# Decode step of two attention-and-MLP layers: extra matmuls over a resident weight at the end of each layer, and one key load cut in two

## The chip, the cores and the metric

The kernel runs on one core of a Trainium2 chip. The metric is device time in microseconds (us) of one execution. TensorE (PE) multiplies, VectorE (DVE) and ScalarE (ACT) work on vectors, GpSimd (POOL) does one small power, SyncE (SP) and ScalarE also issue DMAs. PSUM is the memory that matmuls write; everything else on the core lies in SBUF.

## The reference

One token of width 640 passes twice through the same two blocks, with the same weights and the same cache:

```python
x = x + A_ref(layernorm(x))     # 32 heads of 128 over 8192 cached keys and values, then wo
x = x + B_ref(layernorm(x))     # relu(x @ w1) @ w2, width 1728
x = x + A_ref(layernorm(x))
x = x + B_ref(layernorm(x))
```

`A_ref` is `q = x @ wq` (640 by 4096), scores `q . k * 128**-0.5`, a softmax over the 8192 keys of each head, the weighted sum of the values, and the product with `wo` (4096 by 640). All is float32. The cache is 32 heads x 8192 x 128 x 4 bytes, twice (keys and values): 268 MB. It doesn't fit in SBUF, so it is read from HBM in both layers.

## The kernel before

**Layers and heads.** `attention_and_mlp(L, xr, s)` runs twice. Layer 0 takes the heads from 0 to 31, layer 1 from 31 to 0, so that the last heads of layer 0 are the first of layer 1. What heads 30 and 31 left in SBUF (all of head 31, most of head 30) is used again without a load.

**Ring.** Keys and values go through one SBUF tile, `ring`. `UNITS` says in which units a head is loaded: most heads as one unit of keys and one of values (4 MB each), heads 1 and 29 in halves (2 MB), head 31 in halves of keys and smaller pieces of values. A unit of keys holds runs `(r, 0, 512)` of `K_ALL`, four of them per head. `pump` (L126) issues loads on SP's queue strictly in the order of `todo`, each as soon as `place` finds room for it; `release` frees the room of a piece when its matmuls have been issued, and the load's issue then waits on SP until these matmuls are done. When layer 0 ends, the ring is full of kept pieces and nothing can be loaded until layer 1 has used the first of them. The head that layer 1 loads first is head 29, then head 28. The rest of head 30's keys goes into two weight tiles that are free by then (`load_beside`, L140).

**One head.** `scores` (L336) multiplies four column strips of the array at once: 16 matmuls of 512 columns for a head. Then come the softmax on DVE and ACT, `turn` (L357, transposes by matmul), `rows_weighed` (L370, L377), `values` (L391, again 16 matmuls) and `output` (L415). A float32 matmul shows in the trace as two records.

**End of a layer.** After the last head's `output`, one chain runs that nothing overlaps: the last column times the hidden-layer weights and `wo` (L477, L304), copies to SBUF, turning rows into columns with small matmuls (L643, L656, L664), `deviations` (L261) for the second layer norm, 40 matmuls over `w2` (L304), of which DVE does the first block itself (L651, L684), `spread_of_rows` (L274, then L217 and the power on POOL), and the new `x` (L700). In layer 0 the next layer's `centred` (L232 to L246), `spread_of_columns` (L256), `queries` (L284 to L299) and the first scores follow. In layer 1 the output is stored (L709).

**Order.** The order of instructions on each engine is that of the code. Each engine takes its instructions in turn, and semaphores hold an instruction until its operands are ready. Side jobs (queries of the next group, `wo` of the last, products of `w1` with the last head's rows of `wo`, L464) are generators that are advanced between pieces. `ps_m` gives one PSUM buffer for each name (`pm`, `pt`, `px`, `acc`).

Of the kernel before, what the change touches and what calls it, by code (L numbers as in the profile page):

```python
# [10 lines left out]
F32 = mybir.dt.float32  # L11
# [4 lines left out]
P = 128  # L16
# [19 lines left out]
K_ALL = [(r, 0, RUN) for r in range(4)]  # L36
V_ALL = [(b, 0, 4) for b in range(NBL)]
WHOLE = [("k", K_ALL), ("v", V_ALL)]
HALVES = [("k", K_ALL[:2]), ("k", K_ALL[2:]), ("v", V_ALL[:2]), ("v", V_ALL[2:])]
LAST = [("v", V_ALL[:2]), ("v", V_ALL[2:3]), ("v", [(3, 0, 3)]), ("v", [(3, 3, 1)])]  # L40
UNITS = {h: WHOLE for h in range(H)}
UNITS[0] = HALVES[:2] + LAST
UNITS[1] = HALVES
UNITS[29] = HALVES
UNITS[30] = [
    ("k", [(0, 432, 80), (1, 0, 80)]),
    ("k", [(0, 0, 432)]),
# [25 lines left out]
def decode_kernel(ctx: ExitStack, tc: tile.TileContext, x, kv, wq, wo, w1, w2, out):  # L73
    nc = tc.nc
# [3 lines left out]
    ps_m = ctx.enter_context(tc.tile_pool(name="ps_m", bufs=1, space=bass.MemoryType.PSUM))  # L78
# [88 lines left out]
    def load_wq(g, queue):  # L167
        wq_t[g] = wts.tile([P, NB, HG * DH], F32, name="wq_t")
        queue.dma_start(wq_t[g], wq[g])
# [5 lines left out]
    xr = work.tile([P, DR], F32, name="xr", bufs=2)  # L175
# [14 lines left out]
    ident = consts.tile([P, P], F32, name="ident")  # L190
# [11 lines left out]
    w1_t = consts.tile([P, NB, DFF], F32, name="w1_t")  # L202
# [12 lines left out]
    def inv_std(ss):  # L215
        v = work.tile([P, 1], F32, name="ln_v")
        nc.vector.tensor_scalar(v, ss, 1.0 / D, EPS, op0=ALU.mult, op1=ALU.add)  # L217
        r = work.tile([P, 1], F32, name="ln_r", bufs=2)
        nc.gpsimd.tensor_tensor(r, v, mhalf, op=ALU.pow)
        return r  # L220

    def at_once(steps):
        while True:
            try:
                next(steps)
            except StopIteration as e:
                return e.value

    def centred(xt, s):

        pt = ps_m.tile([P, 512], F32, name="pm")
        nc.tensor.matmul(pt[:, :4], xt[:, :P], sel[:, :4], start=True, stop=True)  # L232
        for g in range(4):
            nc.tensor.matmul(
                pt[32 * g : 32 * g + 32, 4:5],
                xt[:, P:],
                sel[:, g : g + 1],
                start=True,
                stop=True,
            )  # L240
        nc.tensor.matmul(pt[:, 5:6], all_rows, s, start=True, stop=True)
        yield "dve"
        m = work.tile([P, 1], F32, name="ln_m")
        nc.vector.tensor_scalar(m, pt[:, 5:6], 1.0 / D, 0.0, op0=ALU.mult, op1=ALU.add)
        xc = work.tile([P, NB], F32, name="ln_xc", bufs=2)
        nc.vector.tensor_scalar(xc, pt[:, :NB], m, 0.0, op0=ALU.subtract, op1=ALU.add)  # L246
        return xc

    def spread_of_columns(xc):
        sq = work.tile([P, NB], F32, name="ln_sq")  # L250
        ss = work.tile([P, 1], F32, name="ln_ss")
        nc.vector.scalar_tensor_tensor(
            sq, xc, 1.0, xc, op0=ALU.mult, op1=ALU.mult, accum_out=ss
        )
        pv = bank_tile()[:, :1]
        nc.tensor.matmul(pv, ss.to_broadcast([P, P]), ones, start=True, stop=True)  # L256
        return inv_std(pv)
# [14 lines left out]
    def spread_of_rows(ss):  # L272
        pv = ps_m.tile([P, 512], F32, name="pm")
        nc.tensor.matmul(pv[:, :1], all_rows, ss, start=True, stop=True)  # L274
        return inv_std(pv[:, :1])

    qT = {}

    def queries(g, xc, r):

        pq = ps_m.tile([P, 512], F32, name="px")
        for c in range(NB):
            for j in range(HG):
                nc.tensor.matmul(  # L284
                    pq[32 * j : 32 * j + 32, :DH],
                    xc[:, c : c + 1].to_broadcast([P, 32]),
                    wq_t[g][:, c, j * DH : (j + 1) * DH],
                    start=(c == 0),
                    stop=(c == NB - 1),
                )  # L290
        yield "dve"
        row = work.tile([P, DR], F32, name="q_row")[:, :DH]
        nc.vector.tensor_scalar(row, pq[:, :DH], r[0], SCALE, op0=ALU.mult, op1=ALU.mult)
        yield "pe"
        pt = ps_m.tile([P, 512], F32, name="px")
        nc.tensor.matmul(pt[:, :HG], row, sel[:, :HG], start=True, stop=True)  # L296
        yield "dve"
        qT[g] = work.tile([P, HG], F32, name="qT", bufs=2)
        nc.vector.tensor_copy(qT[g], pt[:, :HG])  # L299

    def times_rows(acc, wt, col, first, last):

        for g in range(4):
            nc.tensor.matmul(  # L304
                acc[32 * g : 32 * g + 32, :DR],
                col.to_broadcast([col.shape[0], 32]),
                wt[:, g * DR : (g + 1) * DR],
                start=first,
                stop=last,
                skip_group_check=True,  # L310
            )
# [91 lines left out]
    def output(hd, col):  # L403

        oc = work.tile([P, 5, DH], F32, name="p")
        pt = ps_m.tile([P, 512], F32, name="pm")
        if hd.out is hd.out_3:
            nc.vector.tensor_copy(oc[:, :2], hd.out[:, :2])  # L408
            nc.scalar.copy(oc[:, 2:4], hd.out[:, 2:])  # L409
        else:  # L410
            nc.vector.tensor_copy(oc[:, :3], hd.out[:, :3])
            yield
            nc.vector.tensor_copy(oc[:, 3], hd.out_3[:, 3])
        for r in range(4):
            nc.tensor.matmul(  # L415
                pt[:, :1], oc[:, r], hd.w[:, r : r + 1], start=(r == 0), stop=(r == 3)
            )
        nc.vector.tensor_copy(col, pt[:, :1])

# [66 lines left out]
    def attention_and_mlp(L, xr, s):  # L486
# [3 lines left out]
        groups = [run[0] // HG for run in runs]  # L490
        runs[-1] = runs[-1][:-1]

        acc = ps_m.tile([P, 512], F32, name="acc")
        xc = at_once(centred(xr, s))
        r = [spread_of_columns(xc)]
        at_once(queries(groups[0], xc, r))
        load_wq(groups[1], nc.scalar)

        chores, slow = [], []
# [28 lines left out]
        def before_last():  # L528

            projected(acc, runs[-1][2:], o_cols[NG - 1][:, 2:], False, True)  # L530
            yield "dve"
            xp = work.tile([P, DR], F32, name="xr", bufs=2)
            sp = work.tile([P, 1], F32, name="x_s", bufs=2)
            nc.vector.scalar_tensor_tensor(
                xp, acc[:, :DR], 1.0, xr, op0=ALU.mult, op1=ALU.add, accum_out=sp
            )
            yield "pe"
            xpc = yield from centred(xp, sp)
            yield "pe"
            ph = ps_m.tile([P, 512], F32, name="acc")  # L540
            mlp_in.extend([xp, ph])
            for c in range(NB):
                hidden(ph, xpc[:, c : c + 1], w1_t[:, c], c == 0, False)
                if c < NB - 1:
                    yield "pe"
# [31 lines left out]
        for where, h in enumerate(heads):  # L577
            due(h)
            hd = Head(h)
# [19 lines left out]
            if h == last:  # L599
                o = work.tile([P, 1], F32, name="c_ol")  # L600
                rest = output(hd, o)
# [11 lines left out]
            if h == last:  # L613
                at_once(rest)
            else:
                k, j = divmod(where, HG)
                at_once(output(hd, o_cols[k][:, j : j + 1]))
# [5 lines left out]
            load_beside(mix, 0, DFF)  # L623
        pd = ps_m.tile([P, 512], F32, name="pm")
        times_rows(pd, wo_t[last // HG][:, last % HG], o, True, True)

        hr = wct.rearrange("p c d -> p (c d)")[:, : F_ROWS[0]]
        hT = work.tile([P, FB], F32, name="hT")
# [26 lines left out]
        for g in range(2):  # L655
# [4 lines left out]
                start=True,  # L660
                stop=True,
            )
        for g in range(2):
# [4 lines left out]
                start=True,  # L668
                stop=True,
# [10 lines left out]
        for a, b in enumerate(list(range(4, 8)) + [nb, nb + 1] + list(range(8, nb))):  # L680
            if a == 0:
                ss = deviations(x1, s1)
                for d in range(1, 4):
                    nc.vector.scalar_tensor_tensor(  # L684
                        by_rows,
                        w2_t[:, d],
                        hT[:, d : d + 1],
                        by_rows,
                        op0=ALU.mult,
                        op1=ALU.add,  # L690
                    )
            if a == 8:
                r1 = spread_of_rows(ss)
            rows = 2 * half if b == nb + 1 else P
            times_rows(po, w2_t[:rows, b], hT[:rows, b : b + 1], a == 0, False)
        times_rows(po, by_rows, ones, False, True)

        x2 = work.tile([P, DR], F32, name="xr", bufs=2)
        s2 = work.tile([P, 1], F32, name="x_s", bufs=2)
# [5 lines left out]
    s = work.tile([P, 1], F32, name="x_s", bufs=2)  # L705
    nc.vector.tensor_reduce(s, xr, AX.X, ALU.add)
    for L in range(2):
        xr, s = attention_and_mlp(L, xr, s)
# [77 lines left out]
```

## Time and profile before

| | |
|---|---|
| runs | 1376.67, 1378.78, 1383.95 us (median 1378.78) |
| the profiled execution's own time | 1383.71 us |
| its span, first to last instruction | 1381.9 us |
| TensorE busy | 994.1 us (72%) |
| VectorE / ScalarE busy | 181.3 us (13%) / 99.7 us (7%) |
| DMA, mean over the span | 413 GB/s, 571.41 MB |
| mean granted TensorE clock | 0.786 |

Times in the rows are counted from the span's start. A row of the timeline is: start, duration, engine, line, operation, tiles (out<-in), shape, number of records, and in brackets the idle time of that engine just before and what ended it. "PEld" is the load of a matmul's stationary operand, which can run beside an earlier matmul. In the table of windows, PEclk is the mean share of TensorE's full clock that was granted, and DMA the busy share of the 16 DMA engines. In the chain of waits, a row "DMA" is time in which the last thing waited for was a load.

### The profile page before, as it was taken

The numbers are of one execution on the slowest core, as the hardware profiler recorded it, in microseconds if no ns is written. First come the engines' busy times: TensorE is split into PE (matmuls) and PEld (weight loads), VectorE is DVE, ScalarE is ACT, GpSimd is POOL, SyncE is SP. The second block draws the span as 40 slices with busy tenths as digits, with TensorE's granted clock in tenths as the row PEclk, the third lists the DMA queues.
The fourth block names the chain that finished last, engine by engine and source line by source line (L and its number), as shares of the span: only waits on it lengthen the run. The fifth ranks groups of instructions, "written<-read, shape, count | busy, mean of one in ns | idle before, by whom it ended". The sixth has DMA issues, their size and how long they took to land.

```text
span 1381.9 us, 15834 instructions
## 1 busy us (share of the span) xinstructions
PE 994.1 (72%) x7136; PEld 388.8 (28%) x7136; DVE 181.3 (13%) x688; ACT 99.7 (7%) x271; POOL 2.9 (0%) x10
## 2 busy tenths in 40 slices
PE   5564746687777866877788776686778777677768
PEld 2221312232222222232353322232232322232224
DVE  1010101111111111110131111111110101111112
ACT  0000000000000000000000000000000000000000
POOL 0000000000000000000000000000000000000000
PEclk9786777778786887877787878778878788797787
DMA  9999999999999999999948999999999999999994
GB/s 396 432 431 430 429 432 428 432 428 429 432 431 430 432 427 433 431 428 425 428 159 319 431 431 431 428 425 434 429 432 430 428 432 431 430 432 428 431 424 190
DMA packets 26572, 571.41 MB, mean 413 GB/s; under 512 B 2948, under 2 KB 3080, under 8 KB 4616
## 3 DMA queue, kind: packets, MB, share of 16 engines
q1 hardware_dynamic: 21896, 524.02, 88.6%
q10 hardware_dynamic: 4608, 46.37, 8.1%
q8 instruction: 56, 0.92, 0.3%
q14 instruction: 12, 0.10, 0.0%
HBM read 570.38 MB, written 0.00 MB: 413 GB/s over the span
## 4 chain that ended last, share of the span: by engine, by line
DMA 70%; PE 27%; DVE 1%; ACT 1%; issue 0%; SPq 0%; ACTq 0%; DVEq 0%
DMA ring<-in_kv 70%; PE outs L391 10%; PE ps L336 9%; PE px L464 1%; PE pt L357 1%; PE px L284 1%; PE acc L304 1%; PE px L304 1%; PE acc L477 1%; ACT p L349 1%; PE pm L415 1%; DVE h_t L347 1%; PE pm L377 0%; DVE pT L365 0%; PE px L296 0%
## 5 line engine op out<-in xcount | busy, mean ns | idle before, releaser
L336 PE MATMUL ps<-ring,spread_q 128*32 128x512 f32 (+1 forms) x2056 | 330.3, 769 | 198.3 <-DMA ring<-in_kv 197.8
L391 PE MATMUL outs<-ring,pT 128*4 128x512 f32 (+2 forms) x2128 | 335.2, 784 | 49.3 <-DMA ring<-in_kv 48.9
L336 PEld LDWEIGHTS ps<-ring,spread_q 128*32 128x32 f32 x2056 | 66.6, 133 | 343.2 <-DMA ring<-in_kv 206.8
L391 PEld LDWEIGHTS outs<-ring,pT 128*4 128x4 f32 x2128 | 59.8, 103 | 265.0 <-issue 207.5
L347 DVE TENSOR_REDUCE h_t<-ps 128x1 f32<-128x512 f32 x64 | 44.3, 692 | 492.6 <-PE ps L336 492.6
L349 ACT ACTIVATE p<-ps,h_t 128x512 f32<-128x512 f32 x64 | 44.0, 687 | 701.2 <-DVE h_t L347 689.8
L415 PE MATMUL pm<-h_t,p 128*128 128x1 f32 x512 | 69.0, 256 | 35.1 <-DVE p L408 34.2
L415 PEld LDWEIGHTS pm<-h_t,p 128*128 128x128 f32 x512 | 63.5, 192 | 97.7 <-DVE p L408 96.1
L357 PE MATMUL pt<-row_of,p 128*128 128x16 f32 x512 | 69.9, 269 | 23.4 <-ACT p L349 23.3
L357 PEld LDWEIGHTS pt<-row_of,p 128*128 128x128 f32 x512 | 63.7, 195 | 35.3 <-ACT p L349 35.3
L408 DVE COPY p<-outs 128x256 f32<-128x256 f32 x62 | 26.3, 425 | 350.3 <-PE outs L391 350.3
L370 PE MATMUL pm<-ident,h_t 128*128 128x128 f32 x128 | 31.5, 328 | 44.3 <-DVE h_t L347 44.3
L409 ACT COPY p<-outs 128x256 f32<-128x256 f32 x62 | 23.1, 373 | 486.6 <-DVE p L408 486.6
L370 PEld LDWEIGHTS pm<-ident,h_t 128*128 128x128 f32 x128 | 19.2, 188 | 102.0 <-DVE h_t L347 99.5
L464 PE MATMUL px<-w_t,wct 128*128 128x448 f32 (+1 forms) x80 | 45.5, 654 | 0.0
L377 PE MATMUL pm<-h_t 128*128 128x1 f32 x128 | 27.6, 285 | 24.5 <-DVE h_t L374 24.5
L284 PE MATMUL px<-wq_t,ln_xc 128*32 128x128 f32 x640 | 33.9, 388 | 1.8 <-DMA wq_t<-in_wq 1.8
L284 PEld LDWEIGHTS px<-wq_t,ln_xc 128*32 128x32 f32 x640 | 29.1, 164 | 20.5 <-issue 17.1
L304 PE MATMUL acc<-wo_t,o_cols 128*32 128x160 f32 x496 | 34.2, 443 | 0.0
L377 PEld LDWEIGHTS pm<-h_t 128*128 128x128 f32 x128 | 22.1, 217 | 30.8 <-DVE h_t L374 30.8
L304 PEld LDWEIGHTS acc<-wo_t,o_cols 128*32 128x32 f32 x496 | 23.6, 167 | 24.5 <-issue 18.5
L365 DVE COPY pT<-pt 128x64 f32<-128x64 f32 x64 | 14.4, 225 | 74.2 <-PE pt L357 74.2
(103 smaller groups left out, 240.8 us busy)
## 6 DMA issues: line engine op xcount, KB each, us to landing
ring<-in_kv SPq DMA_DIRECT2D x108, 4096.0 KB, 25.4
ring<-in_kv SPq DMA_DIRECT2D x27, 2048.0 KB, 27.2
wq_t<-in_wq ACTq DMA_DIRECT2D x14, 1280.0 KB, 17.5
wo_t<-in_wo ACTq DMA_DIRECT2D x14, 1280.0 KB, 17.9
w_t<-in_w ACTq DMA_DIRECT2D x1, 4480.0 KB, 25.6
w_t<-in_w ACTq DMA_DIRECT2D x1, 4320.0 KB, 26.1
ring<-in_kv SPq DMA_DIRECT2D x3, 1024.0 KB, 26.4
ring<-in_kv SPq DMA_DIRECT2D x1, 2912.0 KB, 29.2
```

What stands on the lines that cost most here:

```text
L284: nc.tensor.matmul(pq[32 * j : 32 * j + 32, :DH], xc[:, c : c + 1].to_broadcast([P, 32]), wq_t[g][:, c, j * DH : (j + 1) * DH], start=(c = ...
L304: nc.tensor.matmul(acc[32 * g : 32 * g + 32, :DR], col.to_broadcast([col.shape[0], 32]), wt[:, g * DR : (g + 1) * DR], start=first, stop=last,
L336: nc.tensor.matmul(hd.ps[32 * g : 32 * g + 32, c : c + n], spread_q[:, 3 - r : 35 - r], tile_of[:, at + g * n : at + (g + 1) * n], start=f ...
L347: nc.vector.tensor_reduce(hd.nm, hd.ps, AX.X, ALU.max, negate=True)
L349: nc.scalar.activation(hd.p, hd.ps, AF.Exp, bias=hd.nm, scale=1.0, accum_out=hd.l)
L357: nc.tensor.matmul(pt[:, 16 * b : 16 * b + 16], hd.p[:, b * P : (b + 1) * P], row_of.rearrange("p g r -> p (g r)"), start=True, stop=True,)
L370: nc.tensor.matmul(pt[:, :P], hd.nm.to_broadcast([P, P]), ident, start=True, stop=True)
L377: nc.tensor.matmul(pt[:, :1], hd.l.to_broadcast([P, P]), hd.wi, start=True, stop=True)
L391: nc.tensor.matmul((hd.out if r0 < 3 else hd.out_3)[32 * g : 32 * g + 4, r0:r1].rearrange("p r d -> p (r d)"), hd.pT[:, 4 * i : 4 * i + 4] ...
L408: nc.vector.tensor_copy(oc[:, :2], hd.out[:, :2])
L415: nc.tensor.matmul(pt[:, :1], oc[:, r], hd.w[:, r : r + 1], start=(r == 0), stop=(r == 3))
L464: nc.tensor.matmul(pt[:, :n], wct[:, c], w1_t[:, c, f : f + n], start=(c == 0), stop=(c == NB - 1),)
```

## The change

A function `in_wait(n)` is added. It multiplies `n` columns of `w1_t` (loaded in layer 0 and kept) with the identity into a PSUM buffer `pt` that nobody reads. It is called at these places, in the order of TensorE's instructions: `n` = 384 before the last head's `output` matmuls, 192 before the hidden rows are turned to columns, both in each layer; and between the layers 448 after the last `w2` matmuls, 448 in `centred`, 384 and 256 in `queries`. The four between the layers run once, the other two in both layers: eight in all. The last head's `output` matmuls get 64 equal columns in place of one; the first is used. Head 29's first unit of keys (two runs, 2 MB) becomes two units of one run (1 MB) each, in both layers.

```diff
-UNITS[29] = HALVES
+UNITS[29] = [("k", K_ALL[:1]), ("k", K_ALL[1:2])] + HALVES[1:]
...
-    def centred(xt, s):
+    def centred(xt, s, wait=False):
...
         nc.tensor.matmul(pt[:, 5:6], all_rows, s, start=True, stop=True)
         yield "dve"
+        if wait:
+            in_wait(448)
         m = work.tile([P, 1], F32, name="ln_m")
...
+    def in_wait(n):
+
+        pt = ps_m.tile([P, 512], F32, name="pt")
+        nc.tensor.matmul(pt[:, :n], ident, w1_t[:, 0, :n], start=True, stop=True)
...
             nc.vector.tensor_copy(oc[:, 3], hd.out_3[:, 3])
+            in_wait(384)
+        n = 1 if hd.out is hd.out_3 else 64
         for r in range(4):
             nc.tensor.matmul(
-                pt[:, :1], oc[:, r], hd.w[:, r : r + 1], start=(r == 0), stop=(r == 3)
+                pt[:, :n],
+                oc[:, r],
+                hd.w[:, r : r + 1].to_broadcast([P, n]),
+                start=(r == 0),
+                stop=(r == 3),
             )
...
-        xc = at_once(centred(xr, s))
+        xc = at_once(centred(xr, s, L == 1))
         r = [spread_of_columns(xc)]
-        at_once(queries(groups[0], xc, r))
+        first = queries(groups[0], xc, r)
+        next(first)
+        if L:
+            in_wait(384)
+        next(first)
+        next(first)
+        if L:
+            in_wait(256)
+        at_once(first)
         load_wq(groups[1], nc.scalar)
...
         times_rows(pd, wo_t[last // HG][:, last % HG], o, True, True)
+        in_wait(192)
...
         times_rows(po, by_rows, ones, False, True)
+        if L == 0:
+            in_wait(448)
```

The order on TensorE at the end of layer 0, from the last values to the `w2` matmuls. Before:

```order
L391 MATMUL outs_115<-ring,pT 4x128 x4
L415 MATMUL pm<-h_t,p 128x1 x4
L477 MATMUL acc<-mix,c_ol 32x448 x2
L477 MATMUL acc<-mix,c_ol 32x416 x2
L304 MATMUL pm<-wo_t,c_ol 32x160 x4
L643 MATMUL pt<-sel,wct 128x4
L643 MATMUL ps<-sel,wct 128x4 x2
```

With the change (`w_t` is `w1_t`):

```order
L398 MATMUL outs_115<-ring,pT 4x128 x4
L282 MATMUL pt<-w_t,ident 128x384
L424 MATMUL pm<-h_t,p 128x64 x4
L490 MATMUL acc<-mix,c_ol 32x448 x2
L490 MATMUL acc<-mix,c_ol 32x416 x2
L311 MATMUL pm<-wo_t,c_ol 32x160 x4
L282 MATMUL pt<-w_t,ident 128x192
L665 MATMUL pt<-sel,wct 128x4
L665 MATMUL ps<-sel,wct 128x4 x2
```

Two added matmuls stand ahead of instructions that wait for a copy, and the output matmuls are 64 columns wide. The same stands at the end of layer 1.

The order on TensorE between the layers, from the last `w2` matmul to layer 1's first scores. Before:

```order
L304 MATMUL px<-p,ones 32x160 x4
L232 MATMUL pm<-sel,xr 128x4
L234 MATMUL pm<-sel,xr 32x1 x4
L241 MATMUL pm<-x_s,sel 128x1
L256 MATMUL ps<-ones,ln_ss 128x1
L284 MATMUL px<-wq_t,ln_xc 32x128 x20
L296 MATMUL px<-sel,q_row 128x4
L336 MATMUL ps<-ring,spread_q 32x512 x16
```

With the change:

```order
L311 MATMUL px<-p,ones 32x160 x4
L282 MATMUL pt<-w_t,ident 128x448
L232 MATMUL pm<-sel,xr 128x4
L234 MATMUL pm<-sel,xr 32x1 x4
L241 MATMUL pm<-x_s,sel 128x1
L282 MATMUL pt<-w_t,ident 128x448
L258 MATMUL ps<-ones,ln_ss 128x1
L291 MATMUL px<-wq_t,ln_xc 32x128 x20
L282 MATMUL pt<-w_t,ident 128x384
L303 MATMUL px<-sel,q_row 128x4
L282 MATMUL pt<-w_t,ident 128x256
L343 MATMUL ps<-ring,spread_q 32x512 x16
```

Each of the four added matmuls stands ahead of one that waits for DVE.

SP's queue between the layers, from the two loads beside the ring to the first whole units of layer 1. Before:

```order
L140 DMA mix<-in_kv 128x1728
L140 DMA wct<-in_kv 128x640
L126 DMA ring<-in_kv 128x4096 x4
L126 DMA ring<-in_kv 128x8192 x54
```

With the change:

```order
L140 DMA mix<-in_kv 128x1728
L140 DMA wct<-in_kv 128x640
L126 DMA ring<-in_kv 128x2048 x2
L126 DMA ring<-in_kv 128x4096 x3
L126 DMA ring<-in_kv 128x8192 x54
```

Head 29's first load is now held by one run of head 31's keys and not by two; all later loads are held by the same pieces as before.

## The prediction

> **What bounds the kernel now.** I read the page first: its slices, then the shares of the chain.
>
> ```profile
> PEclk9786777778786887877787878778878788797787
> DMA  9999999999999999999948999999999999999994
> DMA 70%; PE 27%; DVE 1%; ACT 1%; issue 0%; SPq 0%; ACTq 0%; DVEq 0%
> ```
>
> Loads bound the kernel except in slices 21 and 22 (where layer 0 ends) and in the last. TensorE's clock is below full nearly everywhere, which costs nothing while loads set the pace. So I looked at windows around the two layer ends, cut where the granted clock changes, and at SP's waits there (680 to 800 us).
>
> ```profile
> core 0: us, PE busy (x) PEld busy (x) DVE busy (x) ACT busy (x) POOL busy (x), PEclk, DMA share, GB/s
> 705.22:708.63 3.41, 2.43 (x32) 1.41 (x24) 1.36 (x5) 0.00 (x0) 0.00 (x0) 1.00 0.00 0
> 708.63:715.46 6.83, 6.80 (x80) 4.90 (x80) 4.67 (x15) 0.37 (x2) 0.00 (x0) 0.50 0.52 178
> 715.46:718.87 3.41, 2.41 (x46) 1.72 (x38) 0.90 (x5) 0.00 (x0) 0.56 (x1) 1.00 0.02 5
> 718.87:729.11 10.24, 8.93 (x72) 4.16 (x76) 1.05 (x7) 0.00 (x0) 0.55 (x1) 0.50 0.46 150
> 732.53:739.35 6.82, 6.43 (x32) 1.69 (x35) 0.83 (x5) 0.00 (x0) 0.00 (x0) 0.50 1.04 423
> 749.50:755.00 5.50, 4.95 (x32) 1.18 (x24) 0.42 (x1) 0.35 (x1) 0.00 (x0) 0.69 0.04 15
> 755.00:1364.00 609.00, 449.36 (x3144) 172.54 (x3148) 77.08 (x288) 45.96 (x126) 0.00 (x0) 0.80 1.00 428
> 1370.82:1377.65 6.83, 6.83 (x81) 4.60 (x80) 4.43 (x13) 0.03 (x1) 0.00 (x0) 0.50 0.00 0
> SPq L126 <- PE outs L391: 33.4, 5, 13.5
> ```
>
> Two things are to be seen. First, loads stop when layer 0 ends and stop again from 749.5 to 755.0 (share 0.04); from 755.0 to 1364.0 they never stop (share 1.00). SP's wait of 13.5 us for L391 is the second stop: head 28's keys need the room of the last of head 30's values. So what layer 1 costs is counted from the moment TensorE ends head 30's values, at 754.1 (below): every microsecond that TensorE saves between 705 and 754 is saved in the end. After 1364 there are no loads left and TensorE's chain is the end itself. Second, in both stretches the clock is at 0.50 most of the time, in steps of 3.41 us.
>
> What takes the clock down? These rows count columns. Four records of a strip matmul run side by side and are one pass.
>
> ```profile
> 500.09 1.90 PE L391 MATMUL outs<-ring,pT 128*4 128x512 f32 x16
> 500.42:503.83 3.41, 2.63 (x24) 1.19 (x16) 0.58 (x2) 0.37 (x1) 0.00 (x0) 1.00 0.98 423
> 503.83:507.24 3.41, 0.00 (x0) 0.00 (x0) 0.00 (x0) 0.00 (x0) 0.00 (x0) 1.00 1.03 442
> 707.16 0.94 PE L477 MATMUL acc<-mix,c_ol 128*32 128x448 f32 x8 [0.25 <-DVE c_ol L418]
> 707.89 0.48 PE L304 MATMUL pm<-wo_t,c_ol 128*32 128x160 f32 x8
> ```
>
> At 500.42 a window held 16 records, 4 passes of 512, less the third of a microsecond before it: about 1,650 columns, and the clock stayed at 1.00 for the next window. The window 705.22:708.63 held 2x448 + 2x160 = 1,216 and a few single ones, and the clock fell, though TensorE was "busy" 2.43 us in it (2.63 in the window that held). So by these rows it is columns that count, with the line between 1,220 and 1,650 in 3.41 us.
>
> [...]
>
> **The change part by part.** The added matmuls put columns into such windows: 768 + 64 x 8 more around 705 to 708, so 2,500. If that holds the clock, these rows become their full-clock forms:
>
> ```profile
> 708.66 0.59 PE L643 MATMUL pt<-sel,wct 128*128 128x4 f32 x2 [0.29 <-DVE wct L633]
> 1370.50 0.39 PE L643 MATMUL pt<-sel,wct 128*128 128x4 f32 x2 [0.29 <-DVE wct L633]
> 711.06 4.67 PE L304 MATMUL px<-w_t,hT 128*32 128x160 f32 x64
> 715.98 0.75 PE L304 MATMUL px<-w_t,hT 128*32 128x160 f32 x16
> 711.95 2.72 DVE L684 SCALAR_TENSOR_TENSOR p<-w_t,hT,p 128x640 f32<-128x640 f32 x3
> 716.08 0.16 DVE L217 TENSOR_SCALAR ln_v<-pm 128x1 f32<-128x1 f32 x1 [1.41 <-PE pm L274]
> 717.13 0.39 DVE L700 SCALAR_TENSOR_TENSOR xr<-px,ln_r,xr 128x160 f32<-128x160 f32 x1 [0.89 <-PE px L304]
> 719.17 0.58 PE L256 MATMUL ps<-ones,ln_ss 128*128 128x1 f32 x2 [0.72 <-DVE ln_sq L252]
> 719.68 2.36 PE L284 MATMUL px<-wq_t,ln_xc 128*32 128x128 f32 x40
> 756.49 1.27 PE L284 MATMUL px<-wq_t,ln_xc 128*32 128x128 f32 x40
> 722.59 0.59 PE L296 MATMUL px<-sel,q_row 128*128 128x4 f32 x2 [0.55 <-DVE q_row L293]
> 723.64 6.39 PE ps L336 x32
> 403.24 3.69 PE ps L336 x32
> ```
>
> (a) Rows to columns, 708.66 to 711.06: 2.40 us. By the two L643 rows a full clock takes 0.39/0.59 = 0.66 of it, 1.58. Gain 0.82.
>
> (b) `w2`, 711.06 to L700 at 717.13: 6.07 us. At full clock ten groups of 0.375 (0.75/2), L274 at 0.4, the last group 0.46 and 0.1 to L700: 4.7. DVE alone allows no less: L684 ends 3.61 after 711.06 and L217 to L700 takes 1.05, together 4.66. Gain 1.37; DVE is the bound then.
>
> (c) Queries: L256 and L296 0.2 each by the L643 ratio, L284 2.36 - 1.27 = 1.09. Gain 1.49.
>
> (d) Head 31's scores: 6.39 - 3.69 = 2.70.
>
> Together 6.38 on layer 0's end.
>
> **What the added matmuls cost.** Each starts when TensorE falls idle and can outlast the wait:
>
> ```profile
> 471.09 0.90 PE px L464 x2
> 705.86 1.05 PE L415 MATMUL pm<-h_t,p 128*128 128x1 f32 x8 [0.47 <-DVE p L411]
> 717.58 0.39 PE L232 MATMUL pm<-sel,xr 128*128 128x4 f32 x2 [0.59 <-DVE xr L700]
> 723.64 3.64 PE L336 MATMUL ps<-ring,spread_q 128*32 128x512 f32 x16 [0.47 <-DVE spread_q L326]
> ```
>
> A matmul of 448 columns between others took 0.90 us at full clock (L464, the nearest form), so 384 takes 0.77, 256 0.51, 192 0.39. Against the waits in brackets: 384 before L415 0.77 - 0.47 = 0.30; 192 before L643 0.10; 448 before L232 nothing, since in (b) TensorE then has DVE's way to L700 and more to wait; 448 before L256 0.18; 384 before L296 0.22; 256 before L336 0.04. In all 0.84. Behind each waits only TensorE's own next instruction; DVE and ACT wait on earlier matmuls. Below, all could be 0: a start a little earlier, with weights loaded beside the last matmul, hides them. I take 0.84. The 64-column output matmuls cost nothing: eight weight loads set L415's 1.05 us, not columns. Layer 0's end gains 5.5.
>
> **Heads 31 and 30** have no added matmuls, and the clock falls in their softmax waits or not, by where the 3.41 us windows lie.
>
> ```profile
> 733.77 6.39 PE outs L391 x40
> 748.82 5.29 PE outs L391 x32
> 864.34 3.66 PE outs L391 x32
> ```
>
> Their values (the last ending at 754.1) lost 2.73 + 1.63 = 4.36 here. The windows will lie otherwise, so the loss can be anything from 0 to twice 2.73 = 5.46; I take the middle, which is 1.63 less than now. Gain of layer 0's end: 7.1, from 4.4 to 9.9.
>
> **Can loads follow?** Head 29 and the next `wq` are 8,192 + 1,280 KB, 9.7 MB, at the 428 GB/s of the row above 22.7 us; the `wq` load can start about 4 us before its 722.1 of now, so all lands near 742. Head 30's values then end near 747. Loads still stop for some 4 us, so the gain is not cut. For the same reason the split load brings nothing: it starts 1 MB one run (0.9 us at full clock) earlier into a stretch that ends in idle DMA engines, and two more issues on an SP that is waiting cost nothing either. If that idle time were gone, the split would be worth up to 0.9 us.
>
> **The end of layer 1.** L643 there ran at full clock, the rest from 1370.82 at half.
>
> ```profile
> 1372.64 4.81 PE L304 MATMUL px<-w_t,hT 128*32 128x160 f32 x64
> 1378.96 0.38 DVE L700 SCALAR_TENSOR_TENSOR xr<-px,ln_r,xr 128x160 f32<-128x160 f32 x1 [0.89 <-PE px L304]
> ```
>
> (a) again: 1370.50 to 1372.64 is 2.14, to 1.58: 0.56. (b): 6.32 to 4.7: 1.62. Less 0.30 + 0.10 for the two added matmuls: 1.8, from 0.6 (both at half clock, 1.55) to 2.2 (no delay).
>
> **Sum.** 7.1 + 1.8 = 8.9 us. The profiled execution took 1383.71 (span 1381.9, 1.8 around it), so it would take 1374.8. It is 4.9 slower than the median of the runs shown; nothing in the sum hangs on that, so the median goes to 1378.78 - 8.9, some **1370 us**. From the bounds of its terms (4.4 + 0.6 to 9.9 + 2.2, so 5.0 to 12.1 gained) and one more on each side for how runs scatter, its own range is 1366 to 1375.
>
> **Rivals.** About 0.5% (6.9 us, the bound at 1371.9) is what a measurement of this kernel can tell from no change.
>
> *The clock is held only in part.* Between the 192 columns, ending near 708.5, and the first `w2` group, near 710.1, no columns are added. A window that begins at 708.5 gets 1.8 us of `w2` at 320 columns per 0.375 us: some 1,530, inside the gap between 1,220 and 1,650 where I can't tell. If the clock falls there, half of (b) and one long added matmul at half speed are lost, about 2 us at each layer's end: 8.9 - 4 = 4.9, 1374 us. For it speaks that the waits without columns are long; against it that only one position of the windows in four or so meets it. Also a bad draw on heads 31 and 30 gives this time.
>
> *The added matmuls run at half clock and delay.* If the clock has fallen when they start, they take twice as long: 1.54 - 0.47, 0.77 - 0.29, 1.80 - 0.59, 1.80 - 0.72, 1.54 - 0.55, 1.03 - 0.47: 5.4 us between the layers, 1.55 at the end, and nothing gained: 1386, slower by 0.5%. It decides if fewer than about 1,220 columns remain in the first window, at 705 to 708; the count of 2,500 speaks against it.
>
> *The clock does not follow columns.* Then it falls as before, at other moments, and the change costs its 0.84 + 0.40: 1380.0. [...]
>
> **How the numbers follow.** The forecast gets 0.62, the clock held in part 0.24, columns not counting 0.08, half-clock delays 0.06. Of the forecast four fifths lie under 1371.9 (0.49), of the clock held in part a quarter (0.06): faster 0.55. Of the delays two thirds lie over 1385.7: slower 0.04. Same: 0.41. The range from 1365 to 1378 leaves out the two last rivals and the ends of the first.
>
> **What would show it.** In the changed profile: PEclk 1.00 from the last values of each layer to the first scores of layer 1; L284's row there at about 1.3 us and head 31's scores at 3.7; from the end of layer 0's values to the end of head 31's scores (705.2 to 730.0, 24.8 us now) about 19.3; from there to the end in layer 1 (1367.1 to 1379.3) about 10.4; loads still idle before head 28's keys. Wrong would be a clock of 0.50 in either stretch, an added matmul of 1.5 us, or loads that never stop between head 29 and head 28: then the loads and not TensorE set that point.

## The result and the profile after

The changed kernel took 1372.72 us (median of 6 runs, 1370.58 to 1374.57) against 1378.76 (6 runs, 1376.67 to 1383.95). The ratio is 0.9947, interval 0.9926 to 0.9967: 7 us faster, from 4.6 to 10.2. The profiled execution took 1372.80 us, its span is 1371.0; that of before took 1383.71.

The slices of the page, as shown of before:

```profile
PEclk8676768887787778877899877787778877787879
DMA  9999999999999999999958999999999999999995
```

Loads still stop only in slices 21, 22 and the last. The windows of the changed kernel: from the end of layer 0's values to the end of head 31's scores; the two in which the clock fell to half after that; the stop of the loads ahead of head 28's keys; the stretch in which loads never stop; and the end of layer 1, from the copy of the last head's output to the last vector instruction.

```profile
704.52:723.28 18.76, 18.24 (x236) 10.62 (x230) 7.92 (x30) 0.37 (x2) 1.10 (x2) 1.00 0.41 146
726.55:729.96 3.41, 3.41 (x18) 0.69 (x21) 0.53 (x3) 0.00 (x0) 0.00 (x0) 0.50 1.08 452
740.20:743.62 3.42, 3.37 (x18) 1.06 (x22) 0.54 (x3) 0.00 (x0) 0.00 (x0) 0.50 0.94 402
743.50:747.00 3.50, 2.94 (x28) 0.96 (x18) 0.42 (x1) 0.37 (x1) 0.00 (x0) 0.98 0.34 94
747.00:1355.00 608.00, 450.57 (x3146) 171.75 (x3149) 77.16 (x288) 45.92 (x125) 0.00 (x0) 0.79 1.00 428
1358.01:1367.91 9.90, 9.19 (x140) 6.14 (x134) 6.12 (x20) 0.37 (x2) 0.55 (x1) 1.00 0.01 2
```

The clock is 1.00 in the whole of both stretches that got matmuls. The first takes 18.8 us in place of 24.8, the last 9.9 in place of 11.9. The loads' pause before head 28's keys is there as before, some 8 us earlier and shorter (5.5 us at a share of 0.04 before, 3.5 us at 0.34 now).

The timeline of the changed kernel, the rows of TensorE and VectorE that answer to those of the sum:

```profile
704.59 0.91 PE L282 MATMUL pt<-w_t,ident 128*128 128x384 f32 x2
705.33 1.00 PE L424 MATMUL pm<-h_t,p 128*128 128x64 f32 x8
706.59 0.94 PE L490 MATMUL acc<-mix,c_ol 128*32 128x448 f32 x8 [0.25 <-DVE c_ol L431]
707.73 0.59 PE L282 MATMUL pt<-w_t,ident 128*128 128x192 f32 x2
708.38 0.39 PE L665 MATMUL pt<-sel,wct 128*128 128x4 f32 x2
710.02 2.65 PE L311 MATMUL px<-w_t,hT 128*32 128x160 f32 x64
711.83 1.80 DVE L706 SCALAR_TENSOR_TENSOR p<-w_t,hT,p 128x640 f32<-128x640 f32 x2
713.55 0.15 DVE L217 TENSOR_SCALAR ln_v<-pm 128x1 f32<-128x1 f32 x1
714.37 0.39 DVE L724 SCALAR_TENSOR_TENSOR xr<-px,ln_r,xr 128x160 f32<-128x160 f32 x1 [0.67 <-POOL ln_r L219]
716.75 1.30 PE L291 MATMUL px<-wq_t,ln_xc 128*32 128x128 f32 x40
719.57 3.64 PE L343 MATMUL ps<-ring,spread_q 128*32 128x512 f32 x32
726.70 5.22 PE L398 MATMUL outs<-ring,pT 128*4 128x512 f32 x40
740.77 5.00 PE L398 MATMUL outs<-ring,pT 128*4 128x512 f32 x32
```

Where the sum's terms came out, counted from the copy that follows layer 0's last values (705.24 before, 704.52 after):

| us | before | predicted | after |
|---|---|---|---|
| (a) rows to columns | 2.40 | 1.58 | 1.64 |
| (b) `w2` to the new `x` | 6.07 | 4.7 | 4.35 |
| (c) 40 records of the query matmuls | 2.36 | 1.27 | 1.30 |
| (d) head 31's scores | 6.39 | 3.69 | 3.64 |
| gain to the end of head 31's scores | | 5.5 | 6.05 (24.81 to 18.76) |
| values of heads 31 and 30, over 3.66 each | 4.36 | 2.73 | 2.90 |
| gain to the end of head 30's values | | 7.1 | 7.56 (48.89 to 41.33) |
| gain at the end of layer 1 | | 1.8 | 1.97 (11.88 to 9.91) |

7.56 + 1.97 = 9.5 against 8.9 predicted. The two profiled executions differ by 10.9: the copy came 0.72 earlier, the loads' stretch took 0.79 less, and 0.14 went the other way behind the last vector instruction. The medians differ by 6.0. That gap between profile and medians is a question to the runs below as well.

### The profile page after: what moved, and what is told of

Read it like the earlier page. It is cut to its first block, busy times and chain, and to the rows that moved or that the text cites. A ratio compares the mean times of both kernels' runs of the same rounds, so it can differ in the third digit from the quotient of the medians.

```text
span 1371.0 us, 15871 instructions
## 1 busy us (share of the span) xinstructions
PE 996.8 (73%) x7152; PEld 388.4 (28%) x7152; DVE 181.4 (13%) x688; ACT 99.7 (7%) x271; POOL 2.9 (0%) x10
## 4 chain that ended last, share of the span: by engine, by line
DMA 70%; PE 27%; DVE 1%; ACT 1%; issue 0%; SPq 0%; POOLq 0%; ACTq 0%; DVEq 0%
DMA ring<-in_kv 70%; PE outs L398 10%; PE ps L343 10%; PE px L477 2%; PE pt L364 1%; PE acc L311 1%; PE px L291 1%; ACT p L356 1%; DVE h_t L354 1%; PE acc L490 1%; PE pm L384 1%; PE pt L282 0%; PE pm L424 0%; PE px L311 0%; DVE pT L372 0%
## 5 line engine op out<-in xcount | busy, mean ns | idle before, releaser
L343 PE MATMUL ps<-ring,spread_q 128*32 128x512 f32 (+1 forms) x2056 | 334.6, 779 | 194.0 <-DMA ring<-in_kv 194.0
L424 PE MATMUL pm<-h_t,p 128*128 128x1 f32 (+1 forms) x512 | 68.1, 255 | 34.3 <-DVE p L415 34.3
L477 PE MATMUL px<-w_t,wct 128*128 128x448 f32 (+1 forms) x80 | 46.5, 667 | 0.0
```

The costliest lines, as they stand in the source:

```text
L343: nc.tensor.matmul(hd.ps[32 * g : 32 * g + 32, c : c + n], spread_q[:, 3 - r : 35 - r], tile_of[:, at + g * n : at + (g + 1) * n], start=f ...
L424: nc.tensor.matmul(pt[:, :n], oc[:, r], hd.w[:, r : r + 1].to_broadcast([P, n]), start=(r == 0), stop=(r == 3),)
L477: nc.tensor.matmul(pt[:, :n], wct[:, c], w1_t[:, c, f : f + n], start=(c == 0), stop=(c == NB - 1),)
```

## The experiments

In all of them lengths are taken from the same points as in the table. An interval stands with each run that was timed more than once; the kernel before ran beside each, and the ratio is to it.

**1 and 2. The split load, taken away and alone.** In the first, `UNITS[29] = HALVES` stands again. In the second the split stays and:

```diff
     def in_wait(n):
+        return
...
-        n = 1 if hd.out is hd.out_3 else 64
+        n = 1
```

> All added matmuls, head 29's first keys as one load again. If the split load is hidden in idle DMA time (the prediction's step), the time is the changed kernel's, about 1372.5, within 1 us; stretches on TensorE as in the changed kernel: 18.8 us from the end of layer 0's values to the end of head 31's scores. If the split carries part of the gain, it is slower by up to 0.9 us, the time of one run of keys, and the loads of head 29 end later by as much.

> The split load alone, no added matmuls, one-column output matmuls. Hidden load: the time of the kernel before, 1378.8, within 1.5 us. If the split carries the gain: 1373 to 1376. The clock falls to 0.50 inside both layer ends in either case, and head 31's scores take about 6.4 us.

Without the split: 1372.55 us (8 runs, 1370.74 to 1374.11), ratio 0.9933 (0.9906 to 0.9960); 18.77 us to the end of head 31's scores, 41.17 to that of head 30's values. With the split alone: 1381.36 us (12 runs, 1375.06 to 1386.78) against 1378.99, ratio 0.9996 (0.9969 to 1.0024). So the added matmuls carry the gain, and no part of it is to be seen from the split. The median of the split alone lies 2.6 us over the 1378.8 that were expected within 1.5; the scatter of these runs is 11.7 us, and the interval of the ratio holds 1.

The second run's profile has the kernel's old end of layer 0 again, but the clock's windows lie elsewhere. In that execution:

```profile
709.33:712.74 3.41, 3.41 (x50) 2.20 (x50) 3.09 (x10) 0.00 (x0) 0.00 (x0) 0.50 0.75 305
712.74:719.57 6.83, 4.98 (x106) 3.75 (x98) 2.06 (x10) 0.00 (x0) 1.10 (x2) 1.00 0.01 2
719.57:722.98 3.41, 2.95 (x17) 0.81 (x21) 0.33 (x2) 0.00 (x0) 0.00 (x0) 0.50 0.87 333
720.14 5.03 PE L342 MATMUL ps<-ring,spread_q 128*32 128x512 f32 x32 [0.46 <-DVE spread_q L332]
1340.80:1354.45 13.65, 12.52 (x72) 5.15 (x68) 1.30 (x6) 0.37 (x1) 0.00 (x0) 0.50 0.99 418
```

Two windows at half clock in place of five: 20.81 us to the end of head 31's scores, not 24.81, with the same instructions there. So without added matmuls this stretch loses 2.05 us against the changed kernel in one execution and 6.05 in another. Head 31's scores took 5.03 us, not the 6.4 expected: the clock was at half only up to 722.98, for the first 2.8 us of them. In the same execution the clock was at half for 13.65 us while the last loads came in, and the copy of the last head's output came 4.3 us after the last landing (1.45 in the profile of before).

**3. As busy, but without columns.** Each added matmul is replaced by one to three of a single column, and the output matmuls have one column again:

```diff
-        nc.tensor.matmul(pt[:, :n], ident, w1_t[:, 0, :n], start=True, stop=True)
+        for i in range(round(n / 160)):
+            nc.tensor.matmul(pt[:, i : i + 1], ident, w1_t[:, 0, i : i + 1], start=True, stop=True)
```

> In place of each added matmul one, two or three of a single column with the same weights (192: one, 256 and 384: two, 448: three), and one-column output matmuls: TensorE is about as busy in the waits, with 1 column in place of hundreds. If the clock follows columns, it falls to 0.50 in both layer ends as before, and the time is the kernel before's plus delays of 0 to 2 us: 1378 to 1381. [...]

1380.39 us (10 runs, 1378.12 to 1384.06), ratio 1.0001 (0.9977 to 1.0025): the whole gain is gone. To the end of head 31's scores it took 23.96 us (18.76 with the change). The windows at the two layer ends of this kernel, each ahead of one at half clock, and for comparison one of the changed kernel that held:

```profile
706.30:709.71 3.41, 3.22 (x50) 2.50 (x46) 2.15 (x11) 0.37 (x2) 0.00 (x0) 1.00 0.51 150
709.71:713.13 3.42, 3.42 (x56) 1.91 (x48) 2.98 (x6) 0.00 (x0) 0.00 (x0) 0.50 0.54 210
1361.66:1365.07 3.41, 3.09 (x31) 2.21 (x31) 1.38 (x6) 0.17 (x1) 0.00 (x0) 1.00 0.00 0
1365.07:1371.90 6.83, 6.83 (x80) 4.80 (x80) 4.46 (x15) 0.19 (x2) 0.00 (x0) 0.50 0.01 2
```

```profile
706.07:709.48 3.41, 2.98 (x31) 1.78 (x30) 1.38 (x8) 0.37 (x2) 0.00 (x0) 1.00 0.28 49
709.48:712.90 3.42, 3.42 (x76) 2.56 (x74) 3.19 (x10) 0.00 (x0) 0.00 (x0) 1.00 0.77 311
```

TensorE was busy 3.22 of 3.41 us and the clock fell; in the changed kernel it was busy 2.98 and the clock held. So neither busy time nor the absence of idle time holds it.

**4. The end of layer 1 alone.** A flag lets the added and the wide matmuls through only after layer 1's first queries; one load for head 29's first keys.

```diff
     def in_wait(n):
+        if not filling[0]:
+            return
...
+        filling[0] = L == 1
         load_wq(groups[1], nc.scalar)
```

> The added matmuls (384 and 192) and the wide output matmuls at the end of layer 1 alone; no split, nothing at the end of layer 0 or between the layers. By the sum of the prediction 1.8 us of the 8.9 come from here: 1377.0 against 1378.8, from the start of the last head's copy to the last vector instruction 9.9 us in place of 11.9. If the end of layer 1 carried more (the chain behind it has nothing beside it), 1374 to 1375.

1380.44 us (10 runs, 1372.65 to 1384.54) against 1378.99, ratio 0.9985 (0.9957 to 1.0013): a gain of 2 us can't be told by these times, and the median is 3.4 us over the 1377.0 expected. The profile can tell it, since by chance its layer 0 runs exactly as that of before (18.40, 24.81, 34.94 and 48.89 us to head 31's first scores, its last, its values, head 30's values, in both):

```profile
1365.70:1375.61 9.91, 9.19 (x140) 6.14 (x134) 6.12 (x21) 0.37 (x2) 0.55 (x1) 1.00 0.01 3
```

It took 9.91 us against 11.88. The term of 1.8 is 1.97.

**5 and 6. The next waits too, with and without the split.** Matmuls go into the softmax waits of layer 1's heads 31 and 30; they write another PSUM buffer (`px`), since `pt` is in use there.

```diff
+            held = L == 1 and where < 2
+            if held:
+                hold(448)
             next(weighing)
+            if held:
+                hold(128)
             turn(hd)
             next(weighing)
+            if held:
+                hold(192)
             next(weighing)
```

> The changed kernel, and matmuls of 448, 128 and 192 columns over the same weight in the softmax waits of layer 1's first two heads (31 and 30) as well. In the changed kernel their values took 5.22 and 5.00 us where 3.66 is full clock. If columns hold the clock there too, both take 3.7 and head 30's values end 2.9 us earlier after layer 0's values, less 0.2 to 0.8 for delays: 38.5 to 39.1 in place of 41.3. Loads of head 29 stopped 3.5 us before head 28's began, so there is just room for that: 1370 against 1372.5. If the loads bind instead, the DMA engines no longer stop there and the time is less than 1 us under the changed kernel's.

> As the run before with head 29's first keys as one load. If there the loads have come to bind, the first of them starts one run of keys later and the time is 0.5 to 0.9 us longer than with the split; if TensorE still sets the point at which head 28's keys are issued, the two agree within 0.3 us in the profile's stretches.

With the split 1370.79 us (12 runs, 1368.94 to 1373.23), ratio 0.9918 (0.9895 to 0.9941); without 1370.62 (12 runs, 1368.97 to 1373.48), ratio 0.9931 (0.9907 to 0.9956). That is 1.9 and 2.1 us under the changed kernel's median, which was taken apart from these. Head 30's values end at 38.08 us in both, in place of 41.33 and somewhat before the 38.5 to 39.1 expected. The last of these rows of run 5 is the stretch in which the loads paused in the changed kernel:

```profile
726.81 3.62 PE L403 MATMUL outs<-ring,pT 128*4 128x512 f32 x40
739.07 3.62 PE L403 MATMUL outs<-ring,pT 128*4 128x512 f32 x32
722.97:743.00 20.03, 18.85 (x168) 8.53 (x164) 4.45 (x17) 2.52 (x7) 0.00 (x0) 1.00 0.99 418
742.50:745.00 2.50, 1.95 (x20) 1.27 (x20) 0.58 (x2) 0.37 (x1) 0.00 (x0) 1.00 0.85 243
```

The values are at full clock, and loads run from 723 to 743 with hardly a pause (0.99, then 0.85 where 0.34 stood). TensorE and the loads reach head 28's keys almost together now, and of the 3.25 us on TensorE some 2 came through in the medians. Where loads are this close to binding the split could have been worth up to 0.9 us; the two runs don't show any.

**7 and 8. Twice, and half the columns.**

```diff
-        nc.tensor.matmul(pt[:, :n], ident, w1_t[:, 0, :n], start=True, stop=True)
+        for i in range(2):
+            nc.tensor.matmul(pt[:, :n], ident, w1_t[:, i, :n], start=True, stop=True)
```

```diff
     def in_wait(n):
+        n = n // 2
...
-        n = 1 if hd.out is hd.out_3 else 64
+        n = 1
```

> Every added matmul of the changed kernel twice. The delay is what of the second one a wait doesn't hide. If the waits were already full, as the prediction has it, each second one costs its whole length: 0.75 + 0.4 + 0.85 + 0.75 + 0.5 = 3.2 us from layer 0's values to head 31's scores (448 after w2 less, since DVE is later there), 18.8 to 22.0 or so, and 1.2 us at the end of layer 1, 9.9 to 11.1. If half of each wait was still free, half of that.

> Half the columns in each added matmul, and one-column output matmuls. By columns, the window with layer 0's last products has some 1,216 + 384 + 192 = 1,800 and holds; the one between w2 and the queries has about 1,600, on the line. So the clock may fall once between the layers (19 to 24 us to the end of head 31's scores, in place of 18.8), and where it falls the window must hold under 1,650 columns, where it holds more than 1,220. If the number of added matmuls counted and not their columns, nothing would change: 18.8 or less.

Doubled: 22.19 us to the end of head 31's scores, 3.43 more, and 10.88 at the end of layer 1, 0.97 more. Rows of the doubled kernel:

```profile
704.44 1.56 PE L283 MATMUL pt<-w_t,ident 128*128 128x384 f32 x4
705.83 1.00 PE L425 MATMUL pm<-h_t,p 128*128 128x64 f32 x8
```

The second 384 columns move L425 by the whole of their 0.65 us: the change's lengths already fill the waits. Halved: 18.31 us, 0.45 less than the change, with the clock at 1.00 up to 724.84; but at the end of layer 1 it fell, and that stretch took 12.8 us. The halved kernel:

```profile
707.77:711.19 3.42, 3.30 (x67) 2.66 (x68) 2.82 (x12) 0.05 (x1) 0.00 (x0) 1.00 0.91 311
711.19:724.84 13.65, 11.97 (x152) 6.79 (x148) 4.50 (x15) 1.07 (x3) 1.10 (x2) 1.00 0.52 196
709.27 2.65 PE L312 MATMUL px<-w_t,hT 128*32 128x160 f32 x64
1363.14:1366.55 3.41, 3.10 (x32) 2.15 (x31) 0.98 (x6) 0.37 (x2) 0.00 (x0) 1.00 0.00 0
1366.55:1380.37 13.82, 8.58 (x104) 5.50 (x103) 4.92 (x16) 0.00 (x0) 0.55 (x1) 0.50 0.01 1
```

In the window 707.77:711.19 the clock held. It contains 1.92 us of the `w2` matmuls, whose 64 records are 16 passes of 160 columns in 2.65 us: some 1,850 columns. The window 1363.14:1366.55 contains the last products (1,216) and 96 columns in two passes, 1,408 in all, and the clock fell. In this kernel the line lies between these two counts. With half the columns it depends on where the windows lie whether the clock holds. Each of the two kernels was timed once, and the times (1379.58 and 1380.13) carry no verdict.

**9 and 10. The last heads of layer 1.** In the first, run 6's kernel gets `hold(448)` also ahead of head 1's pieces that wait for a load and ahead of head 0's first keys, and the three in head 1's softmax waits; in the second these stand alone, without any of the others.

```diff
+                if L and where >= H - 2 and a % 2 == 0 and (h != last or a == 0):
+                    hold(448)
                 scores(hd, piece, at, a == 0, a == len(pieces) - 1)
...
+            held = L == 1 and (where < 2 or where == H - 2)
...
+                if L and where == H - 2 and a == 2:
+                    hold(448)
                 values(hd, piece, at, a == 0, a == len(pieces) - 1)
```

> Head 29's first keys as one load, the changed kernel's added matmuls, those in the softmax waits of heads 31 and 30 of layer 1, and further ones in layer 1's head 1 and ahead of head 0's first keys, where TensorE waits for loads. From the landing of the last load to the copy of the last head's output the profiles show 0.3 to 0.6 us where the clock held ahead of it and 1.4 to 4.3 where it fell. If the clock there makes the rest of the scatter from run to run, this stretch is 0.3 to 0.6 and the runs lie within 3 us of each other, 1369 to 1372, median 1370. If it doesn't, the median stays at 1370.7 and the scatter at 1369 to 1373.5.

> Only the matmuls in layer 1's head 1 and ahead of head 0's first keys; none of the change's, one-column output matmuls, one load. If they take nothing but the slow ends (4.3 us between last landing and last copy), the median falls by 0 to 2 us against the kernel before and the scatter of 12 us stays for the most part, since the end of layer 0 makes it: head 30's values ended 43.5 to 48.9 us after layer 0's values in the profiles without added matmuls there. If the ends of layer 1 make the scatter, it shrinks to 5 us or less.

All together: 1369.63 us (6 runs, 1369.08 to 1371.76), ratio 0.9933 (0.9910 to 0.9957). The clock of its profile, from layer 0's last values to head 30's, and from 1337 to the end:

```profile
704.00:746.00 42.00, 40.13 (x458) 21.45 (x451) 12.69 (x48) 3.26 (x10) 1.10 (x2) 1.00 0.70 277
1337.00:1367.00 30.00, 27.15 (x330) 14.68 (x328) 9.54 (x34) 1.81 (x6) 0.55 (x1) 1.00 0.51 211
```

The runs lie within 2.7 us, as expected; from the last landing to the last copy it took 0.9 us and not 0.3 to 0.6, though the clock held. Its median is the lowest here, 3.1 us under the changed kernel's, but it was not run beside it, and against runs 5 and 6 it is 1 us, within their scatter. The last heads' matmuls alone: 1376.39 us (10 runs, 1372.61 to 1383.58), ratio 0.9995 (0.9969 to 1.0021), scatter 11 us. So the waits of the last heads do not make the scatter of the kernel before. What takes most of it away is the added columns at the end of layer 0: the kernels with all of them there scatter by 2.7 to 4.5 us (the change, runs 1, 5, 6 and 9), those with none by 11 to 13 (before in 31 runs, runs 2, 4 and 10). Run 3 lies between with 5.9, which stays unexplained.

## Why the prediction was right

The time lies within the range (1372.72, with 1370 forecast), 0.8 us over the 1371.9 under which most of the forecast's chance was put, and the mechanism is the one predicted. Point by point:

- *What bounds the kernel.* Right. The 7.56 us gained up to the end of head 30's values reached head 28's load, since the loads still paused there. When runs 5 and 6 took 3.25 us more from TensorE, the pause was nearly gone, as the estimate of when head 29's loads land implied (742 predicted; the DMA engines fall idle at about 743.5 in the profile after).
- *Columns, not idle time.* Right, by run 3: after a window busy for 94% (3.22 of 3.41 us) without added columns the clock fell, after one busy for 87% (2.98) with them it held. The third rival is out with that. The prediction had the line between 1,220 and 1,650 columns; run 8 raises the lower figure to 1,408.
- *Terms (a) to (d).* All within 0.35 us. (b) was better than forecast, 4.35 us in place of 4.7, and both of its sums were a little too long. L706 did end 3.61 us after the first `w2` matmul (713.63), as the prediction had L684. But L217 starts at 713.55, and from there to the new `x` it took 0.82 us: the 1.05 were read from a row in which the last matmuls ended the wait, and now POOL's power ends it. The ten groups are no bound either: 0.375 us was half of a row of 16 records with its end, while 64 records take 2.65 us, 0.33 for each group of 8.
- *What the added matmuls cost.* 0.84 forecast, some 0.6 measured, if each step of the change is set against the same step at full clock in the profile of before or of run 2. The single terms are off: the 192 columns cost 0.3 and not 0.10 (L490 to L665 takes 1.79 us, and L477 to L643 took 1.50), the 448 before L232 0.13 and not nothing, and the others less than forecast. Halving gave back 0.45 (run 8), and doubling cost 3.43, with 3.2 expected for waits that are full.
- *Heads 31 and 30.* 2.90 lost against 2.73, which was the middle of a range from 0 to 5.46: that it came so near is luck. Run 5 gave it back whole.
- *The split brings nothing.* Nothing speaks against it in three pairs (the change with run 1, before with run 2, run 5 with run 6).
- *The clock held in part.* Not in this profile, nor in those of runs 1, 5, 6 and 9. The 1,530 columns of this rival were too few: 1.8 us of `w2` are some 1,740 by the row of 64 records in 2.65 us, above the 1,650 that held. Run 8's window 707.77:711.19 begins 1.5 us ahead of the first `w2` matmul, about where the rival had it, behind all columns added there, and the clock held. At the end of layer 1 run 8 shows what a fall costs, 2.9 us, with half the columns.
- *Carrying the sum to the median.* Here a step failed in size. The prediction had it that the profiled execution stood 4.9 us over the median and that "nothing in the sum hangs on that". It does: the 17.1 us at half clock from which terms (a) to (d) are counted are one draw of where windows lie. Run 2's profile shows another, with 6.8 us at half clock and 2.05 us to be gained to the end of head 31's scores in place of 6.05. The time before scatters by far more than that of the change: 1374.62 to 1387.21 in 31 runs of the kernel before, 1370.58 to 1374.57 in 6 of the change. So the profile pair gave 10.9 us, the medians 6.0 and the ratio about 7. The 8.9 lies inside the interval of 4.6 to 10.2, on the side to be expected of a sum that is made on an execution 4.9 us over the median. That the forecast came within 2.9 us of the median is in part luck: in run 2's profile the same two places lie only 2.2 and 2.7 us over those of the change (43.52 us to the end of head 30's values, 12.61 at the end of layer 1), 4.9 in place of 9.5.

## What to carry to other kernels

Where a chain of short dependent matmuls is the end of everything, look at the granted clock window by window: a matmul that nobody reads, cut to the length of a wait that is there anyway, can keep the following work at full speed (here for a price of some 0.6 us where 6 were gained in one profile and 2 would have been in another). Here the columns in a window decided and not the busy time (run 3: the clock fell after 3.22 of 3.41 us busy, and in the changed kernel it held after 2.98), so count them, and give the filling no more than the wait (doubled, it cost 4.4 us of the gain); take a gain that comes from such a clock from several executions, since one profile holds one draw of the windows.

## What the runs showed of the hardware that was not expected

How sharp the line is in the profile of before. Its windows of 3.41 us were counted from 16 us on, by the time in which columns stream: passes of 512 columns start 0.43 us apart at full clock and 0.85 at half, other widths in proportion, strips side by side once. The clock fell after 108 windows, all with up to 39% of the window streaming, and held after 118, all with 37% or more. So in this profile the two meet at 37 to 39%; from the 0.43 us for 512 columns that is some 1,500 to 1,600 columns, an estimate. From half clock it rose after 108 windows, all with 77% or more, and stayed after 65, all with 76% or less; from the 0.85 us that is 1,560 to 1,580 columns, also an estimate. One-column matmuls and weight loads did not hold it: in run 3's window 1361.66:1365.07 the products with 1,216 columns are 1.0 us of streaming out of 3.09 us busy, and the clock fell.

The scatter of the kernel from run to run, 12.6 us before and 4.0 after, fits the place of those windows. In the five profiles without added columns at the end of layer 0, head 30's values end 43.5 to 49.0 us after layer 0's last values. The stretch between head 30's values and the last head's copy, where loads bind, took 612.2 to 613.5 us in nine of the twelve profiles; the three with 614.8 to 616.1 are those in which the clock was at half for 8.7 us or more of the 25 us before that copy (6.8 or less in the others): 13.7 us with 616.1 in run 2's, 6.8 with 613.0 in that of before, 3.4 with 612.2 in that of the change. Each kernel has one profile, so how the scatter of the times divides between the two is not shown.
